# One scale for three tokens, a bound from sums, and a block's operand made within one block

## The chip, the cores and the metric

The kernel runs on one core of a Trainium2 chip. TensorE (PE) multiplies matrices into PSUM, VectorE (DVE), ScalarE (ACT) and GpSimd (POOL) do the element work, and SyncE (SP) issues most DMAs. Each engine takes its instructions in program order; between engines, semaphores order them. Measured is the device time of one execution in microseconds (us). The kernel before takes 1029.41 us, the median of three runs (1028.08 to 1030.17).

## The reference

Three stages on 4 batches of 4224 tokens with 192 channels.

```python
out = np.einsum('hk,bskhg->bshg', softmax(weight), windows(x))   # a causal 7-tap filter per head
u = x + (xT @ U @ V)T                                            # token mixing of rank 32
x = u + np.maximum(u @ w_ch1, 0.0) @ w_ch2                       # 192 -> 768 -> 192, first layer pair
u = x + np.real(np.fft.fft(np.fft.fft(x, axis=1), axis=2))
un = (u - mean(u)) / np.sqrt(var(u) + 1e-06)                     # per token
out = u + np.maximum(un @ w_ch1, 0.0) @ w_ch2                    # second layer pair
```

## The kernel before

**Blocks.** Both layer pairs work on blocks of 384 tokens: 128 partitions with three tokens each (`TB` = 3). There are 11 blocks in a batch and 88 in all, (s, b, j): s = 0 for the first layer pair and s = 1 for the second, b the batch. The order is (0,0), (0,1), (0,2), (1,0), (0,3), (1,1), (1,2), (1,3), 11 blocks each, so that blocks 0 to 32 and 44 to 54 have s = 0. Block i is the i-th of them.

**One block's life.** `pre1` (s = 0) or `pre2` (s = 1) makes the operand of the first layer. For s = 0: `add` puts the token mixing on `u` (matmuls `h`, then DVE, L525 or L534), `sizes` sums |u| of each token on ACT (L543), `scales` makes of the sums a scale per token on DVE (`cmax`, `rc`, L547 and L550), `high` scales `u` to `un` (ACT, L555) and rounds it to 16 bits in `sp` (L578), `low` takes the rest `un - sp` on POOL (L561), and a DMA transpose on SP (L585) turns `sp` into `ch`, channels on partitions. There is one buffer for `sp` and two for `ch`. For s = 1 `stats`, `root` and `normal` make mean and root of each token (L596 to L619), then come `high` (L625, L578) and `low` (L631; on DVE for 10 blocks). `layer1` multiplies `ch` with the first weights, six PSUM banks `l`, each evicted by ACT (`hh`, L650) and DVE (`hl`, L651). `layer2` multiplies `hh` and `hl` with the second weights, one token column r at a time (L697, L699, L701), and DVE adds the result to `u` (L704). After the third column of an s = 0 block DVE takes the largest |u| (L712) for the FFT's scale, and SP stores `u` to `x2d`, twice for j < 6; for s = 1 it stores the output.

**The order.** The program is written out by the loop at the end of `build`. In block i's turn r runs from 0 to 2: two of `layer1(i)`'s six units, then one unit of `layer2(i-1)`, then `fill`, which plays a share of the background units: the filter's matmuls and their evictions (`cv`, L398 and L404), the second weights' decoding on DVE (`dec`, L172 to L179), and the FFT (`fold`, `split33`, `s33`, `sd`, `s128`, `adds`), which gathers rows of `x2d` by DMAs that POOL issues (`xm`, L756). The preparation of block i+2 is laid among these: for s = 0 `add` in turn i at r = 0 and 1, `sizes` at r = 1 and 2, `scales` at r = 2, `high` and `low` in turn i+1 at r = 0 (in `PAIRED` stretches, where six `layer1` units stand together at r = 0, at the end of turn i). For s = 1: `stats` at r = 0, `root` and `normal` at r = 1, `high` and `low` at r = 2. `START` orders the first 29 steps by hand.

Of the kernel before, what the change touches and what calls it, by code (L numbers as in the profile page):

```python
# [20 lines left out]
P = 128  # L21
# [21 lines left out]

PAIRED = [(5, 11), (22, 34), (76, 88)]
# [53 lines left out]
def build(tc, io):  # L98
# [30 lines left out]
    with tc.manual_schedule():  # L129
# [319 lines left out]
        vsc = cst.tile([P, 2], F32, name="vsc")  # L449
        vst = cst.tile([96, 12, TB * P], F16, name="vst")  # L450
# [57 lines left out]
        def pre1(b, j):  # L508
            k = blk_t[0, b, j]
            u = k["u"]  # L510
            plain = b not in gst

            def add(r0, n):
                if plain:

                    if r0 == 0:
                        o = []
                        for r in range(TB):
                            t = TB * j + r
# [25 lines left out]
            def scales():  # L545
                c = k["cs"]
                nc.vector.tensor_scalar(out=c, in0=c, scalar1=1e-30, scalar2=1.0 / 8000.0,  # L547
                                        op0=ALU.max, op1=ALU.mult)
                rc = k["rc"] = wrk.tile([P, TB], F32, name="rc")
# [38 lines left out]
        def pre2(b, j):  # L588
# [3 lines left out]
            def stats():  # L592
                st = wrk.tile([P, TB, 6], F32, name="st")
                mv = wrk.tile([P, TB, 2], F32, name="mv", bufs=3)
                for r in range(TB):
                    nc.vector.bn_stats(out=st[:, r], in_=u[:, r])  # L596
                for r in range(TB):
                    nc.vector.bn_aggr(out=mv[:, r], in_=st[:, r])
                v = wrk.tile([P, TB], F32, name="va", bufs=1)
                nc.vector.tensor_scalar(out=v, in0=mv[:, :, 1], scalar1=1e-6, scalar2=None,  # L600
                                        op0=ALU.add)
                k["mv"], k["va"] = mv, v

            def root():
                s = k["s"] = wrk.tile([P, TB], F32, name="sd", bufs=1)
                nc.scalar.activation(s, k["va"], AF.Sqrt)

            def normal():
                mv, v, s = k["mv"], k["va"], k["s"]
                r = wrk.tile([P, TB], F32, name="rs", bufs=1)  # L610
                nc.vector.reciprocal(r, s)
                nc.vector.tensor_tensor(out=s, in0=r, in1=r, op=ALU.mult)
                nc.vector.scalar_tensor_tensor(out=s, in0=s, scalar=-16.0, in1=v,
# [21 lines left out]
            return [(None, stats), (root, normal), (high, low), (None, None)]  # L635
# [46 lines left out]
        def layer2(s, b, j):  # L682
# [6 lines left out]
            def unit(r):  # L689
# [16 lines left out]
                if final:  # L706
                    nc.sync.dma_start(io["out"][b][:, j * TB + r], u[:, r])
# [17 lines left out]
        def fft_units(b):  # L725
# [11 lines left out]
            def scale2():  # L737
# [3 lines left out]
                                        scalar2=2.0 ** -13, op0=ALU.max, op1=ALU.mult)  # L741
                nc.vector.reciprocal(m[:, 13:14], m[:, 12:13])
                nc.vector.tensor_scalar(out=m[:, 14:15], in0=m[:, 12:13], scalar1=2.0 ** 11,
# [63 lines left out]
            def s33(c, e):  # L807
# [17 lines left out]
                for a, n, o in ((1 + 3 * g0, 3 * nn, 0), (0, ng - nn, 102 * nn)):  # L825
                    if n:
# [3 lines left out]
                        nc.scalar.activation(hi, v, AF.Identity, scale=2.0 ** -11)  # L830
                        nc.vector.scalar_tensor_tensor(out=lo, in0=v, scalar=2.0 ** -11, in1=hi,
# [110 lines left out]
        def ahead(i):  # L942
            if i >= nblk:
                return [(None, None)] * 4
# [75 lines left out]
        def play(t):  # L1020
            for q in START[t].split() if t < len(START) else ():
                if q in jobs:
                    jobs[q]()
                else:
                    if q[0] in "ab" and q[0] not in queues:
                        queues[q[0]] = [f for e in ahead("ab".index(q[0])) for f in e]
# [30 lines left out]
        last, pre = None, [(None, None)] * 4  # L1057
        for i in range(nblk + 1):
            l1 = layer1(*blocks[i]) if i < nblk else [lambda: None] * NM
            old, pre = pre, ahead(i + 2)  # L1060

            soon = any(n < nblk and in_pairs(*blocks[n]) for n in (i + 1, i + 2))
            for r in range(TB):
                now = ([old[TB]] if r == 0 else []) + [pre[r]]
                l1[2 * r]()
                l1[2 * r + 1]()
                run(f for f, _ in now)
# [5 lines left out]
                run(f for _, f in now)  # L1073
                fill(TB * i + r)
            if soon:
                run(pre[TB])
                pre = pre[:TB] + [(None, None)]
# [60 lines left out]
```

## Time and profile before

| | |
|---|---|
| median of 3 runs | 1029.41 us (1028.08 to 1030.17) |
| the profiled execution: span from first to last instruction | 1017.3 us (its time beyond the span is not in the profile; the median is 12.1 us above the span) |
| PE busy | 979.1 us, 96% |
| DVE, ACT, POOL busy | 748.4 us (74%), 604.4 us (59%), 380.9 us (37%) |
| DMA engines | 45.6% of the span for the queue of SP and ACT, mean 137 GB/s in all |

PE's busy time counts from a matmul's start to its modelled end, so matmuls overlap: in a full stretch a matmul with 192 columns starts every 0.08 us and one with 384 every 0.16 us. What PE lost shows as idle time, in square brackets behind the instruction that ended it, with the work that released it, and as stretches with a lower granted clock.

### The profile page before, as it was taken

To read this page: it belongs to the slowest core of one execution; us is meant where nothing else is said; L and a number is where in the kernel's file an instruction comes from. 1 tells how busy PE (TensorE), PEld (TensorE's weight loads), DVE (VectorE), ACT (ScalarE), POOL (GpSimd) and SP (SyncE) were. 2 spreads that over 40 slices of the span, in tenths; PEclk is the share of its full clock that TensorE was granted. 3 is DMA by queue.
4 is the path that set the end of the run, shared out by engine and by line. 5 is a ranking of instruction groups with operands and counts; after the bars stand their busy time and mean duration, and the time that the engine had idled before them with its cause. 6 is when DMAs were issued, how large, how long until landed. Compare 5 with 4: busy or idle time off the path is not lost.

```text
span 1017.3 us, 25682 instructions
## 1 busy us (share of the span) xinstructions
PE 979.1 (96%) x9929; PEld 764.8 (75%) x9929; DVE 748.4 (74%) x2094; ACT 604.4 (59%) x1512; POOL 380.9 (37%) x397
## 2 busy tenths in 40 slices
PE   8789898999899999999999999998999999999998
PEld 5466676777677777877778887776888877877776
DVE  7766577689876656687776777897789787766663
ACT  2556554765676666656576666655656665555552
POOL 0111111253552344265534445564157651562110
PEclk9999999999999999999999999999999999999999
DMA  7596857685536666443425455433344332542332
GB/s 288 155 230 183 252 148 189 178 213 158 151 99 154 203 201 179 114 138 101 102 73 146 134 155 139 108 87 82 87 131 110 107 87 65 137 110 68 82 72 63
DMA packets 190804, 139.28 MB, mean 137 GB/s; under 512 B 128186, under 2 KB 164257, under 8 KB 189913
## 3 DMA queue, kind: packets, MB, share of 16 engines
q1 hardware_dynamic: 183095, 124.59, 45.6%
q0 software_dynamic: 7104, 12.70, 4.8%
q8 instruction: 77, 1.26, 0.5%
q14 instruction: 46, 0.38, 0.1%
q10 hardware_dynamic: 482, 0.35, 0.1%
HBM read 61.69 MB, written 46.11 MB: 106 GB/s over the span
## 4 chain that ended last, share of the span: by engine, by line
PE 62%; DVE 12%; DMA 11%; POOL 5%; issue 5%; ACT 4%; SPq 0%; DVEq 0%; ACTq 0%; POOLq 0%
PE l L665 24%; PE l L697 9%; PE l L701 8%; PE l L699 8%; PE l L655 5%; DMA ch<-sp 4%; DVE hl L651 3%; DMA xm<-x2d,mrow 2%; POOL xm L756 2%; PE cv L398 2%; PE sd L863 2%; PE s L879 2%; DMA x1d<-xw 1%; DVE x L790 1%; POOL xp L804 1%
## 5 line engine op out<-in xcount | busy, mean ns | idle before, releaser
L665 PE MATMUL l<-ch,w1h 128*128 128x384 f16 x1584 | 407.2, 327 | 15.4 <-DMA ch<-sp 10.1
L697 PE MATMUL l<-w2h,hh 128*128 128x192 f16 x1584 | 391.9, 247 | 5.8 <-DVE hl L651 4.5
L699 PE MATMUL l<-w2l,hh 128*128 128x192 f16 x1584 | 391.4, 247 | 1.2 <-DVE w2l L264 1.2
L701 PE MATMUL l<-w2h,hl 128*128 128x192 f16 x1584 | 391.4, 247 | 0.5 <-DVE hl L651 0.4
L651 DVE SCALAR_TENSOR_TENSOR hl<-l,hh 128x384 f16<-128x384 f32 x528 | 267.6, 549 | 127.2 <-ACT hh L650 126.1
L650 ACT ACTIVATE hh<-l 128x384 f16<-128x384 f32 x528 | 235.3, 494 | 155.7 <-PE l L655 155.3
L665 PEld LDWEIGHTS <-w1h 128*128 128x128 f16 x1584 | 155.1, 98 | 106.8 <-DMA ch<-sp 12.3
L697 PEld LDWEIGHTS <-hh 128*128 128x128 f16 x1584 | 155.6, 98 | 23.1 <-issue 12.3
L665 PE MATMUL l<-ch,w1l 128*128 128x384 f16 x528 | 172.7, 327 | 0.0
L699 PEld LDWEIGHTS <-hh 128*128 128x128 f16 x1584 | 155.7, 98 | 17.1 <-issue 6.5
L701 PEld LDWEIGHTS <-hl 128*128 128x128 f16 x1584 | 155.7, 98 | 3.1 <-DVE hl L651 1.4
L561 POOL TENSOR_TENSOR sp<-un,sp 128x576 f16<-128x576 f32 x44 | 57.3, 1302 | 250.4 <-ACT sp L578 228.3
L655 PE MATMUL l<-ch,w1l 128*128 128x384 f16 (+1 forms) x528 | 133.9, 327 | 0.0
L756 POOL DMA_INDIRECT xm<-x2d,mrow x84 | 84.9, 1011 | 21.3 <-issue 17.8
L631 POOL TENSOR_TENSOR sp<-un,sp 128x576 f16<-128x576 f32 x34 | 44.9, 1320 | 120.2 <-ACT sp L578 118.9
L625 ACT ACTIVATE un<-u,mr,rs 128x192 f32<-128x192 f32 x132 | 62.4, 537 | 25.3 <-DVE mr L619 24.7
L555 ACT ACTIVATE un<-u,rc 128x192 f32<-128x192 f32 x132 | 50.2, 445 | 43.0 <-DVE rc L550 43.0
L704 DVE SCALAR_TENSOR_TENSOR u<-l,cmax,u 128x192 f32<-128x192 f32 x132 | 54.5, 413 | 25.5 <-PE l L701 20.9
L665 PEld LDWEIGHTS <-w1l 128*128 128x128 f16 x528 | 51.8, 98 | 28.0 <-issue 4.0
L543 ACT ACTIVATE junk<-u 128x192 f16<-128x192 f32 x132 | 47.7, 361 | 40.6 <-DVE u L534 24.2
L849 POOL DMA_INDIRECT u<-x2d,mrow x64 | 62.4, 975 | 15.3 <-issue 11.7
L704 DVE SCALAR_TENSOR_TENSOR u<-l,ws,u 128x192 f32<-128x192 f32 x132 | 53.9, 410 | 18.2 <-PE l L701 18.0
(136 smaller groups left out, 1189.5 us busy)
## 6 DMA issues: line engine op xcount, KB each, us to landing
x2d<-u SPq DMA_DIRECT2D x68, 288.0 KB
u<-x1d SPq DMA_DIRECT2D x44, 288.0 KB
out_d<-u SPq DMA_DIRECT2D x43, 288.0 KB
x1d<-xw SPq DMA_DIRECT2D x36, 210.0 KB
u<-x2d SPq DMA_DIRECT2D x32, 192.0 KB
x<-x2d SPq DMA_DIRECT2D x60, 99.0 KB
xw<-x_d SPq DMA_DIRECT2D x4, 1344.0 KB
xw<-x_d SPq DMA_DIRECT2D x8, 672.0 KB
```

The costliest lines, as they stand in the source:

```text
L561: low_engine(0, b, j).tensor_tensor(out=sp[:, :, D:2 * D], in0=k["un"], in1=sp[:, :, :D], op=ALU.subtract)
L625: nc.scalar.activation(un[:, t], u[:, t], AF.Identity, scale=k["r"][:, t:t + 1], bias=k["m"][:, t:t + 1])
L650: nc.scalar.activation(hh[:, m], acc[m], AF.Relu)
L651: nc.vector.scalar_tensor_tensor(out=hl[:, m], in0=acc[m], scalar=0.0, in1=hh[:, m], op0=ALU.max, op1=ALU.subtract)
L655: nc.tensor.matmul(acc[m].rearrange("p (r n) -> p r n", r=TB), lhsT=w["l1"][rows, n, m * P:(m + 1) * P], rhs=kd[x][rows], start=False, sto ...
L665: nc.tensor.matmul(o, lhsT=w[v][:, e, ms], rhs=kd[x], start=(n == 0), stop=False)
L697: nc.tensor.matmul(o, lhsT=hh[:, m, rs], rhs=w["h2"][:, m], start=(m == 0), stop=False)
L699: nc.tensor.matmul(o, lhsT=hh[:, m, rs], rhs=w["l2"][:, m], start=False, stop=False)
L701: nc.tensor.matmul(o, lhsT=hl[:, m, rs], rhs=w["h2"][:, m], start=False, stop=(m == NM - 1))
L704: nc.vector.scalar_tensor_tensor(out=u[:, r], in0=o, scalar=sc, in1=u[:, r], op0=ALU.mult, op1=ALU.add)
L756: nc.gpsimd.indirect_dma_start(out=xs[c][1][:, g], out_offset=None, in_=x2d[b][:], in_offset=bass.IndirectOffsetOnAxis(ap=mrow[:99, k:k + ...
L849: nc.gpsimd.indirect_dma_start(out=u2[:, s0 + 2 * e], out_offset=None, in_=src[:], in_offset=bass.IndirectOffsetOnAxis(ap=mrow[:, k2 + e - ...
```

## The change

The turn of a block now has twelve slots: slot 4r comes after the first `layer1` unit of r, 4r + 1 after the second, 4r + 2 after `layer2`'s unit, 4r + 3 after `fill`. `SLOTS` says in which slot each piece of the preparation of block i+2 stands, and no number in it reaches 12.

- s = 0: one scale for a partition's three tokens. `sizes`, `scales` and `high` become one instruction each over 576 elements, where `sizes` and `high` had three. `add` stands in slot 5, `sizes` and `scales` in 7, `high` in 9 and `low` in 10.
- s = 1: `stats` in slot 0, `root` and `normal` in 4, `high` and `low` in 9. The constant 1e-6 goes into the root as a bias, and one small DVE instruction (L600) goes.
- `layer2`: the first two columns share a PSUM bank and are added by one DVE instruction of 384 elements after the second; the third as before. The last block's output leaves in two stores, not three.
- The FFT's bound is a sum of |u| by ACT instead of a largest |u| by DVE; two powers of two change with it.

```diff
+SLOTS = [(5, 5, 7, 7, 9, 10), (0, 4, 4, 9, 9)]
...
-            def sizes(r0, n):
-
-                if r0 == 0:
-                    k["cs"] = wrk.tile([P, TB], F32, name="cmax", bufs=5)
-                junk = wrk.tile([P, D], F16, name="junk", bufs=1)
-                for r in range(r0, r0 + n):
-                    nc.scalar.activation(junk, u[:, r], AF.Abs, accum_out=k["cs"][:, r:r + 1])
+            def sizes():
+                k["cs"] = wrk.tile([P, 1], F32, name="cmax", bufs=5)
+                junk = wrk.tile([P, TB * D], F16, name="junk", bufs=1)
+                nc.scalar.activation(junk, u.rearrange("p r d -> p (r d)"), AF.Abs,
+                                     accum_out=k["cs"])
...
-                for r in range(TB):
-                    nc.scalar.activation(un[:, r], u[:, r], AF.Identity,
-                                         scale=k["rc"][:, r:r + 1])
+                nc.scalar.activation(un.rearrange("p r d -> p (r d)"),
+                                     u.rearrange("p r d -> p (r d)"), AF.Identity,
+                                     scale=k["rc"])
...
-            return [(None, lambda: add(0, 2)), (lambda: sizes(0, 2), lambda: add(2, 1)),
-                    (lambda: sizes(2, 1), scales), (high, low)]
+            return list(zip(SLOTS[0], (lambda: add(0, 2), lambda: add(2, 1), sizes, scales, high, low)))
...
-            return [(None, stats), (root, normal), (high, low), (None, None)]
+            return list(zip(SLOTS[1], (stats, root, normal, high, low)))
...
-                ps = psm("l2")
-                o = ps[:, :D]
+                if r != 1:
+                    k["l2"] = psm("l2")
+                o = k["l2"][:, D:2 * D] if r == 1 else k["l2"][:, :D]
...
-                sc = k["cs"][:, r:r + 1] if s == 0 else w["ws"]
-                nc.vector.scalar_tensor_tensor(out=u[:, r], in0=o, scalar=sc, in1=u[:, r],
-                                               op0=ALU.mult, op1=ALU.add)
+                sc = k["cs"] if s == 0 else w["ws"]
+                if r:
+                    a = 2 * (r - 1)
+                    v = u[:, a:r + 1].rearrange("p r d -> p (r d)")
+                    nc.vector.scalar_tensor_tensor(out=v, in0=k["l2"][:, :(r + 1 - a) * D],
+                                                   scalar=sc, in1=v, op0=ALU.mult, op1=ALU.add)
...
-                        nc.vector.tensor_reduce(out=xmax[b][:, j:j + 1],
-                                                in_=u.rearrange("p r d -> p (r d)"), axis=AX.X,
-                                                op=ALU.max, apply_absolute_value=True)
+                        junk = wrk.tile([P, TB * D], F16, name="junk", bufs=1)
+                        nc.scalar.activation(junk, u.rearrange("p r d -> p (r d)"), AF.Abs,
+                                             accum_out=xmax[b][:, j:j + 1])
...
             for r in range(TB):
-                now = ([old[TB]] if r == 0 else []) + [pre[r]]
                 l1[2 * r]()
+                at(4 * r)
                 l1[2 * r + 1]()
-                run(f for f, _ in now)
+                at(4 * r + 1)
                 play(TB * i + r + 1)
...
-                run(f for _, f in now)
+                at(4 * r + 2)
                 fill(TB * i + r)
+                at(4 * r + 3)
```

Three places in the order of the instructions. On POOL before, from the gathers around block 17's preparation on; `un_3687` is block 18's, `xm` the FFT's gathered rows.

```order
L804 TENSOR_TENSOR xp_3523<-xm_2988,xp_3523 99x768
L756 DMA xm_3399<-x2d0_70,mrow_78 99x192 x2
L795 TENSOR_TENSOR xm_3399<-x33_3398 99x4x95
L756 DMA xm_3661<-x2d0_70,mrow_78 99x192 x2
L561 TENSOR_TENSOR sp_84<-un_3687,sp_84 128x3x192
L804 TENSOR_TENSOR xp_3768<-xm_3399,xp_3768 99x768
```

The same place on POOL now; block 18's is `un_3503`.

```order
L806 TENSOR_TENSOR xp_3415<-xm_2897,xp_3415 99x768
L758 DMA xm_3296<-x2d0_70,mrow_78 99x192 x2
L562 TENSOR_TENSOR sp_86<-un_3503,sp_86 128x3x192
L797 TENSOR_TENSOR xm_3296<-x33_3295 99x4x95
L758 DMA xm_3560<-x2d0_70,mrow_78 99x192 x2
L806 TENSOR_TENSOR xp_3653<-xm_3296,xp_3653 99x768
```

The subtraction of block 18 has moved in front of the FFT's `fold` (L795, now L797) and two gathers.

On DVE before, in turn 5, where the second weights' first piece has just been decoded (its last instruction is L223); `rc_1577` is block 7's scale.

```order
L223 TENSOR_REDUCE mx1_1482<-u2_1474 128x1
L122 TENSOR_REDUCE vsc_82<-am_1548 128x1
L464 TENSOR_SCALAR vsc_82<-vsc_82 128x1
L466 RECIPROCAL vsc_82<-vsc_82 128x1
L704 SCALAR_TENSOR_TENSOR u_673<-l2_1553,cmax_902,u_673 128x192
L712 TENSOR_REDUCE xmax_821<-u_673 128x1
L547 TENSOR_SCALAR cmax_1484<-cmax_1484 128x3
L550 RECIPROCAL rc_1577<-cmax_1484 128x3
L651 SCALAR_TENSOR_TENSOR hl_1592<-l1_1593,hh_1591 128x384
```

The same place on DVE now; block 7's scale is `rc_1493`.

```order
L224 TENSOR_REDUCE mx1_1435<-u2_1427 128x1
L548 TENSOR_SCALAR cmax_1489<-cmax_1489 128x1
L551 RECIPROCAL rc_1493<-cmax_1489 128x1
L123 TENSOR_REDUCE vsc_82<-am_1514 128x1
L467 TENSOR_SCALAR vsc_82<-vsc_82 128x1
L469 RECIPROCAL vsc_82<-vsc_82 128x1
L706 SCALAR_TENSOR_TENSOR u_668<-l2_1519,cmax_907,u_668 128x192
L649 SCALAR_TENSOR_TENSOR hl_1549<-l1_1550,hh_1548 128x384
```

The scale stands directly behind the decoded piece, five instructions sooner, and the reduction L712 is no longer on DVE; the decoding is ahead of it as before.

On SP before, at the end of turn 12; `ch_2910` is block 14's operand, `u_1985` block 11.

```order
L716 DMA x2d1_71<-u_1985 128x576 x2
L504 DMA u_2863<-x1d1_67 128x576
L585 DMA_TRANSPOSE ch_2910<-sp_84 128x9x128
L368 DMA x1d2_68<-xw_2119 56x4x192 x2
L773 DMA x33_2987<-x2d0_70 33x4x192 x3
```

The same place on SP now.

```order
L718 DMA x2d1_71<-u_1930 128x576 x2
L585 DMA_TRANSPOSE ch_2778<-sp_86 128x9x128
L507 DMA u_2786<-x1d1_67 128x576
L369 DMA x1d2_68<-xw_2058 56x4x192 x2
L775 DMA x33_2718<-x2d0_70 33x4x192 x3
```

The transpose has moved in front of the load of a later block and stands right behind the two stores.

## Rows read from the trace of the kernel before

**Rows 1.** The page: busy time, share of the span and instructions of three engines.

```profile
PE 979.1 (96%) x9929; PEld 764.8 (75%) x9929; DVE 748.4 (74%) x2094; ACT 604.4 (59%) x1512; POOL 380.9 (37%) x397
```

**Rows 2.** What PE waited for: total us, times, longest us.

```profile
PE l L665 <- DMA ch<-sp: 10.1, 10, 2.8
```

**Rows 3.** PE's timeline: start, us, instruction, in brackets the idle time and its end.

```profile
42.20 0.32 PE L665 MATMUL l<-ch,w1h 128*128 128x384 f16 x1 [2.67 <-DMA ch<-sp]
...
65.78 0.34 PE L665 MATMUL l<-ch,w1h 128*128 128x384 f16 x1 [1.30 <-DVE xmax L712]
...
77.16 0.34 PE L665 MATMUL l<-ch,w1h 128*128 128x384 f16 x1 [0.34 <-DMA ch<-sp]
...
124.86 0.32 PE L697 MATMUL l<-w2h,hh 128*128 128x192 f16 x1 [3.37 <-DVE hl L651]
...
165.34 0.24 PE L697 MATMUL l<-w2h,hh 128*128 128x192 f16 x1 [1.16 <-DVE hl L651]
...
169.74 0.34 PE L665 MATMUL l<-ch,w1h 128*128 128x384 f16 x1 [1.18 <-DMA ch<-sp]
...
193.02 0.44 PE L398 MATMUL cv<-xw,tap 64*64 64x168 f32 x4 [1.03 <-DMA xw<-x_d]
...
267.08 0.50 PE L665 MATMUL l<-ch,w1h 128*128 128x384 f16 x1 [2.83 <-DMA ch<-sp]
...
991.04 0.34 PE L665 MATMUL l<-ch,w1h 128*128 128x384 f16 x1 [0.45 <-DVE u L704]
```

**Rows 4.** Three stretches: us, busy us of PE, PEld, DVE, ACT, POOL, clock, DMA share.

```profile
123.20:130.00 6.80, 5.14 (x42) 3.88 (x42) 4.95 (x10) 4.58 (x11) 1.53 (x2) 0.50 0.69 179
130.00:266.60 136.60, 129.09 (x1393) 100.16 (x1391) 106.71 (x284) 84.39 (x231) 41.91 (x38) 1.00 0.64 172
266.60:270.00 3.40, 2.92 (x10) 1.41 (x11) 2.22 (x9) 0.49 (x1) 1.71 (x2) 0.50 0.93 301
```

**Rows 5.** ACT's timeline at 257 us, block 18's rounding.

```profile
257.07 0.68 ACT L578 ACTIVATE sp<-un 128x576 f16<-128x576 f32 x1
```

**Rows 6.** POOL's timeline from 251 to 264 us.

```profile
251.25 1.00 POOL L756 DMA_INDIRECT xm<-x2d,mrow  x1 [0.30 <-issue]
258.68 1.23 POOL L795 TENSOR_TENSOR xm<-x 99x380 f32<-99x380 f32 x1 [6.43 <-DVE xm L791]
...
262.44 1.30 POOL L561 TENSOR_TENSOR sp<-un,sp 128x576 f16<-128x576 f32 x1
```

**Rows 7.** DVE's timeline in turn 5.

```profile
117.57 0.26 DVE L172 TENSOR_SCALAR dec<-u 128x192 int32<-128x192 int32 x1 [3.41 <-DMA u<-wa_d]
...
119.31 0.35 DVE L223 TENSOR_REDUCE mx<-u 128x1 f32<-128x192 f32 x1
...
121.46 0.17 DVE L550 RECIPROCAL rc<-cmax 128x3 f32<-128x3 f32 x1
```

**Rows 8.** ACT's timeline in turn 5.

```profile
121.72 1.15 ACT L555 ACTIVATE un<-u,rc 128x192 f32<-128x192 f32 x3 [6.64 <-DVE rc L550]
...
123.74 0.47 ACT L650 ACTIVATE hh<-l 128x384 f16<-128x384 f32 x1
```

**Rows 9.** Groups by line and shape: count, busy us, mean ns, idle before us.

```profile
L704 DVE SCALAR_TENSOR_TENSOR u<-l,cmax,u 128x192 f32<-128x192 f32 x132 | 54.5, 413 | 25.5 <-PE l L701 20.9 <-PE gp L414 0.5
L712 DVE TENSOR_REDUCE xmax<-u 128x1 f32<-128x576 f32 x44 | 33.1, 753 | 1.5
L534 DVE SCALAR_TENSOR_TENSOR u<-h,gm,u 128x384 f32<-128x384 f32 x33 | 20.1, 608 | 0.4 <-PE s L879 0.2
...
L578 ACT ACTIVATE sp<-un 128x576 f16<-128x576 f32 x88 | 60.1, 683 | 3.1 <-DMA ch<-sp 0.4
L543 ACT ACTIVATION_READ_ACCUMULATOR junk<-u 128x1 f32 x132 | 25.2, 191 | 0.0
```

**Rows 10.** SP's timeline at 57 us, a transpose's issue.

```profile
57.62 5.38 SPq L585 DMA_TRANSPOSE ch<-sp  x1
```

**Rows 11.** The page's DMA issues: count and KB each.

```profile
x2d<-u SPq DMA_DIRECT2D x68, 288.0 KB
```

More of the change, by code (lines that the diff above doesn't have):

```diff
@@ L449, in build @@
         vsc = cst.tile([P, 2], F32, name="vsc")
+        eps = cst.tile([P, 1], F32, name="eps")
+        nc.gpsimd.memset(eps, 1e-6)
         vst = cst.tile([96, 12, TB * P], F16, name="vst")
@@ L548, in scales @@
                                         op0=ALU.max, op1=ALU.mult)
-                rc = k["rc"] = wrk.tile([P, TB], F32, name="rc")
+                rc = k["rc"] = wrk.tile([P, 1], F32, name="rc")
                 nc.vector.reciprocal(rc, c)
@@ L598, in stats @@
                     nc.vector.bn_aggr(out=mv[:, r], in_=st[:, r])
[L599 to L602, printed above, removed]
+                k["mv"] = mv
             def root():
                 s = k["s"] = wrk.tile([P, TB], F32, name="sd", bufs=1)
-                nc.scalar.activation(s, k["va"], AF.Sqrt)
+                nc.scalar.activation(s, k["mv"][:, :, 1], AF.Sqrt, bias=eps)
             def normal():
-                mv, v, s = k["mv"], k["va"], k["s"]
+                mv, s = k["mv"], k["s"]
                 r = wrk.tile([P, TB], F32, name="rs", bufs=1)
                 nc.vector.reciprocal(r, s)
-                nc.vector.tensor_tensor(out=s, in0=r, in1=r, op=ALU.mult)
-                nc.vector.scalar_tensor_tensor(out=s, in0=s, scalar=-16.0, in1=v,
+                nc.vector.scalar_tensor_tensor(out=s, in0=mv[:, :, 1], scalar=1e-6, in1=r,
+                                               op0=ALU.add, op1=ALU.mult)
+                nc.vector.scalar_tensor_tensor(out=s, in0=s, scalar=-16.0, in1=r,
                                                op0=ALU.mult, op1=ALU.mult)
@@ L702, in unit @@
                                      stop=(m == NM - 1))
-                sc = k["cs"][:, r:r + 1] if s == 0 else w["ws"]
-                nc.vector.scalar_tensor_tensor(out=u[:, r], in0=o, scalar=sc, in1=u[:, r],
-                                               op0=ALU.mult, op1=ALU.add)
-                if final:
-                    nc.sync.dma_start(io["out"][b][:, j * TB + r], u[:, r])
+                sc = k["cs"] if s == 0 else w["ws"]
[4 more added lines that the diff above has]
+                                                   scalar=sc, in1=v, op0=ALU.mult, op1=ALU.add)
+                    if final:
+                        nc.sync.dma_start(io["out"][b][:, j * TB + a:j * TB + r + 1], u[:, a:r + 1])
                 if r == TB - 1:
@@ L740, in scale2 @@
                 nc.vector.tensor_scalar(out=m[:, 12:13], in0=m[:, 12:13], scalar1=1e-30,
-                                        scalar2=2.0 ** -13, op0=ALU.max, op1=ALU.mult)
+                                        scalar2=2.0 ** -14, op0=ALU.max, op1=ALU.mult)
                 nc.vector.reciprocal(m[:, 13:14], m[:, 12:13])
-                nc.vector.tensor_scalar(out=m[:, 14:15], in0=m[:, 12:13], scalar1=2.0 ** 11,
+                nc.vector.tensor_scalar(out=m[:, 14:15], in0=m[:, 12:13], scalar1=2.0 ** 5,
                                         scalar2=None, op0=ALU.mult)
@@ L829, in s33 @@
                                   [:, :, a:a + n] for l in range(2)]
-                        nc.scalar.activation(hi, v, AF.Identity, scale=2.0 ** -11)
-                        nc.vector.scalar_tensor_tensor(out=lo, in0=v, scalar=2.0 ** -11, in1=hi,
+                        nc.scalar.activation(hi, v, AF.Identity, scale=2.0 ** -5)
+                        nc.vector.scalar_tensor_tensor(out=lo, in0=v, scalar=2.0 ** -5, in1=hi,
                                                        op0=ALU.mult, op1=ALU.subtract)
@@ L943, in ahead @@
             if i >= nblk:
-                return [(None, None)] * 4
+                return []
             s, b, j = blocks[i]
@@ L1025, in play @@
                     if q[0] in "ab" and q[0] not in queues:
-                        queues[q[0]] = [f for e in ahead("ab".index(q[0])) for f in e]
+                        queues[q[0]] = [f for _, f in ahead("ab".index(q[0]))]
                     for _ in range(int(q[1:] or 1)):
@@ L1055, in fill, with at @@
                     done[n] = upto
-        last, pre = None, [(None, None)] * 4
+        last, pre = None, []
         for i in range(nblk + 1):
             l1 = layer1(*blocks[i]) if i < nblk else [lambda: None] * NM
-            old, pre = pre, ahead(i + 2)
+            pre = [(n - 12, f) for n, f in pre if n >= 12] + ahead(i + 2)
+            def at(n):
+                run(f for m, f in pre if m == n)
             soon = any(n < nblk and in_pairs(*blocks[n]) for n in (i + 1, i + 2))
             for r in range(TB):
-                now = ([old[TB]] if r == 0 else []) + [pre[r]]
                 l1[2 * r]()
+                at(4 * r)
                 l1[2 * r + 1]()
-                run(f for f, _ in now)
+                at(4 * r + 1)
                 play(TB * i + r + 1)
@@ L1072, in build @@
                     last[r]()
-                run(f for _, f in now)
+                at(4 * r + 2)
                 fill(TB * i + r)
+                at(4 * r + 3)
             if soon:
-                run(pre[TB])
-                pre = pre[:TB] + [(None, None)]
+                run(f for n, f in pre if n >= 12)
+                pre = []
             ahead_load(i + 4)
```

2 rows, old and new, of the table START are left out of this document.

## The prediction

> **What bounds the kernel now.** I read the busy shares first. PE is busy in 96% of the span, DVE in 74%, ACT in 59% [rows 1]. So the change, which takes no matmul away, can only win what PE loses by waiting, 1017.3 - 979.1 = 38.2 us, and what it loses to a lower clock. Second, PE's waits by releaser: 10.1 us in ten waits are for the transposed operand `ch` [rows 2], the largest single releaser. Third, where these waits lie: PE's timeline has six over 1 us that the change may touch, 1.30 us at 65.78, 3.37 at 124.86, 1.16 at 165.34, 1.18 at 169.74, 1.03 at 193.02 and 2.83 at 267.08; behind them come seven under 0.6 us before a block's first matmul, from 0.34 at 77.16 to 0.45 at 991.04, 2.7 us together [rows 3]. Fourth, the granted clock. It is 1.00 nearly everywhere (130.0 to 266.6 is such a stretch), but 0.50, 1.2 GHz for 2.4, from 123.2 to 130.0 and from 266.6 to 270.0, each right at a long idle of PE [rows 3, 4]. Work in these stretches runs at half speed, so they cost half their length, 3.4 and 1.7 us.
>
> **The operand sooner (s = 0).** Take 267.08. ACT had rounded block 18 by 257.07 + 0.68 = 257.75 us [rows 5], but POOL's subtraction began at 262.44: POOL stood in order in front of the FFT's fold, which waited 6.43 us for DVE until 258.68, and two gathers [rows 6]. From the subtraction's end at 263.74 to PE's matmul at 267.08 went 3.3 us. In the changed order the subtraction stands in front of that fold, right behind the gathers that were done at 252.25 [rows 6], and its own inputs are made in the turn before. So it ends some 8 us sooner, the operand lands long before PE asks for it, and the 2.83 us go. What is late next is the eviction of block 17, which DVE makes no later than before. With the idle goes its reason for the low clock, 1.7 us. The waits at 65.78 and 169.74 are the same kind, an operand made just in time: 1.30 + 1.18. PE's wait at 65.78 carries DVE's L712 as releaser; that instruction leaves DVE, and the transpose moves in front of a load on SP, so either cause is gone. Of the seven small waits four lie in s = 0, where the operand comes some half a turn sooner, and three in s = 1, where only `normal` moves; I take 2.2 of their 2.7 us. The xw load that ends the wait at 193.02 was queued on SP behind a transpose that now comes sooner; how far the load's own buffer allows it no row shows, so 0 to 1.03, and I take 0.5. Sum of this part: 2.83 + 1.7 + 1.30 + 1.18 + 2.2 + 0.5 = 9.7 us; bounds 4 (large waits half closed, no clock) and 10.7.
>
> **Less on DVE, in front of the evictions.** In an s = 0 block three additions of 413 ns and a reduction of 753 ns become additions of 608 (the 384-element row of L534) and 413 ns [rows 9]: 1.99 us become 1.02. In an s = 1 block the additions save 0.22. That is 44 x 0.97 + 44 x 0.22 = 52 us of DVE's 748. Off the path it is worth nothing; PE hides it. It counts where DVE sets PE's wait, at 124.86. There DVE waits 3.41 us for the second weights' DMA until 117.57, decodes until 119.66, and reaches block 7's scale at 121.46 [rows 7]; ACT starts `high` at 121.72 and the evictions of block 6 only at 123.74 [rows 8], and PE needs a bank that they free. The scale now stands right behind the decoded piece: 119.66 plus two short instructions, about 120.0. `high` is one instruction instead of three in 1.15 us [rows 8]; the same 576 elements take 683 ns in L578 [rows 9], a per-partition scale may add some, say 0.7. With 0.95 us of rounding ACT is free at 121.7. But in front of the evictions it now has the sum for the bound, 683 + 191 ns [rows 9], and so reaches them at 122.5, 1.2 us sooner. The decoding and its DMA are not moved. Of the 3.37 us 1.2 go (bounds 0.3, if the sum waits for the last column, and 2.1, if it is hidden). The clock's 3.4 us then hang on an idle of 2.2 us: all or nothing, and the nearest rows lie on both sides, 2.83 us with the drop and 2.67 at 42.20 without [rows 3]; I take half, 1.7. At 165.34 the same order, with no DMA, should close all of 1.16. Sum 4.1 us; bounds 1.5 and 6.7.
>
> **What it adds.** The sum for the bound makes ACT wait in every s = 0 block for DVE's last addition; behind it stand the filter's evictions and the next block's first `hh`. PE has by then two further `layer1` units (ten matmuls of 0.16 us) and a `layer2` unit of an older block (18 of 0.08) in its queue, 3 us of work, and that covers 0.87 us. Uncovered it would be 44 x 0.87 = 38 us; with a margin of 2 us per block I take 0. On DVE `scales` now waits for ACT's `sizes` in slot 7; what is queued behind it is the eviction of unit 4, whose `hh` ACT makes after `sizes` anyway: 0. The shared bank is held from column 0 to column 1, but a block takes one bank fewer, and where six units stand together column 0 was evicted only after six `hl` before too: 0. The tail: the last store stands behind a store of two columns rather than one, 0.2 us.
>
> The Trainium skill ("ScalarE: Activation LUTs", Rules for kernel authors) says that a maximum belongs on VectorE, which is faster per element, and so speaks against this move. The rows agree on the price of one, 874 ns for 753, but not on the place: DVE is the fuller engine. If ACT bounded, the rule would make the move cost 44 x 0.12 = 5.3 us and the sum 1022.8.
>
> **The sum.** 9.7 + 4.1 - 0.2 = 13.6 us. PE will reach the waits that the change does not touch (gathers, filter loads) that much sooner, and some will grow; I give back 1.6 and take 12. The profiled span is 1017.3 and would be 1005.3; the median stands 12.1 us above the span, and I carry that over: 1029.4 - 12.0 = 1017.4 us.
>
> **Rivals.** *Half is lost again:* the closed idle comes back as longer waits for gathers, weights and filter loads, whose times DMA sets. For it: DVE's wait in turn 5 is for a DMA [rows 7], and the xw wait is one [rows 3]. Against: the loads are issued in program order behind work that moves with PE. 6 us stay: 1023.4.
>
> *More closes:* both low clocks go, and the relieved DVE shortens the FFT's and the start's waits too. 10.7 + 6.7 and some 3 us more: 20 us, 1009.
>
> *Slower: the transposes queue behind the stores.* In s = 0 the transpose now stands on SP right behind the stores to `x2d`, 2 x 288 KB [rows 11] in the 24 blocks with j < 6. At the 172 GB/s of a usual stretch [rows 4] these 576 KB take 3.3 us. `sp` has one buffer, so a loop runs through every block: stores 3.3, transpose 3.3, rounding 0.68, subtraction 1.30, together 8.6 us against 1017.3 / 88 = 11.6 us for a block. It decides from 3 us more on. For it: one transpose behind other traffic took 5.38 us for its issue alone [rows 10]; 4 us of that, 12.6 for 11.6, would hold ACT's rounding and with it the next evictions 1 us in each of 24 blocks: 24 - 12 = 12 us slower, 1041. Against: that one stood behind the weights' and the filter's first transfers, in the fullest stretch. The Trainium skill ("DMA: Bandwidth & Descriptors", Queues, rings and completion order) has each DMA engine consume descriptors in ring order; by that the 3.3 us are paid in every such block, and whether more is, no row shows.
>
> *It does nothing:* the waits are set by something that the rows name wrongly, as at 65.78, and new ones replace them: 1029.
>
> **Chances.** The forecast's case (7 to 17 us faster) 0.57, half lost 0.18, more closes 0.06, nothing 0.06, slower 0.13. A measurement of this kernel can tell 0.2%, 2.1 us, from no change. Faster by more: 0.57 + 0.18 + 0.06 = 0.81; within: 0.06; slower: 0.13. The likeliest case alone spans 1012 to 1023. The range goes from 1008 (more closes) to 1030, where nothing is still inside and slower is left out.
>
> **What would show it.** Right: in the changed profile no wait over 0.5 us for `ch` after 60 us; POOL's subtraction of block 18 before the fold; PE's clock 1.00 around the former 267 us; the wait behind the first decoded piece near 2 us; DVE's busy time near 696 us and ACT's no higher. Wrong: ACT idle before the sum for the bound with PE idle right behind it; a transpose's issue of several us in most s = 0 blocks, with ACT's L578 waiting for `ch`; or PE's idle as large as before under other releasers.

## The result, and the profile after

The changed kernel takes 1002.77 us, the median of four runs (1000.67 to 1004.68), and the kernel before, beside it, 1029.79 (1028.08 to 1031.99). The ratio is 0.9735, with a 95% interval of 0.9715 to 0.9755: 27 us faster, where 12 were forecast. The direction was right; the time lies below the range.

The page of the changed kernel, busy time by engine, which answers to [rows 1]:

```profile
span 999.7 us, 25272 instructions
PE 972.6 (97%) x9929; PEld 761.5 (76%) x9929; DVE 684.3 (68%) x1918; ACT 593.8 (59%) x1336; POOL 380.9 (38%) x398
```

PE is idle or waiting for 27.1 us of the span, not 38.2, and its busy time fell by 6.5 us with not a matmul fewer; 13.6 us less at 1.2 GHz (the stretches below) would save 6.8. DVE lost 64 us, ACT 11. The profiled execution took 1001.54 us, 1.84 more than its span.

What PE waited for (total us, times, longest), the first of them the line of [rows 2]; the second has no counterpart before, and the third stands in the turn that had 1.16 us at 165.34:

```profile
PE l L663 <- DMA ch<-sp: 2.7, 2, 2.2
...
PE l L698 <- issue: 2.3, 3, 1.1
...
PE h L533 <- DVE hl L649: 1.8, 1, 1.8
```

The 10.1 us in ten waits for `ch` are 2.7 in two, and 2.2 of these stand at 41.52 us, in front of the program's first block. PE's timeline, in the places of [rows 3] and at the largest waits that are left:

```profile
48.92 0.32 PE L663 MATMUL l<-ch,w1h 128*128 128x384 f16 x1 [2.54 <-DVE hl L649]
...
57.55 0.24 PE L698 MATMUL l<-w2l,hh 128*128 128x192 f16 x1 [0.16 <-DVE w2l L265]
...
116.96 0.24 PE L696 MATMUL l<-w2h,hh 128*128 128x192 f16 x1 [0.51 <-DVE hl L649]
...
155.72 0.24 PE L533 MATMUL h<-gst,vst 96*128 96x192 f16 x1 [1.76 <-DVE hl L649]
...
209.87 0.24 PE L698 MATMUL l<-w2l,hh 128*128 128x192 f16 x1 [0.58 <-issue]
...
431.10 0.25 PE L698 MATMUL l<-w2l,hh 128*128 128x192 f16 x1 [1.05 <-issue]
...
675.95 0.43 PE L825 MATMUL s<-vt,xp 99*97 99x102 f16 x5 [1.43 <-POOL xp L806]
```

The waits of 3.37 and 2.83 us are 0.51 and nothing. The 1.16 us at 165.34 have become 1.76, a wait for a PSUM bank that DVE has to empty. New are pieces that no releaser ends ("issue", 5.5 us in all after 38 us), in the middle of runs of matmuls.

The stretches of [rows 4]; columns as there:

```profile
49.86:53.28 3.41, 3.41 (x14) 1.62 (x13) 2.51 (x9) 2.13 (x5) 0.00 (x0) 0.50 0.90 232
53.28:998.70 945.42, 928.83 (x9484) 734.01 (x9482) 644.65 (x1814) 573.85 (x1290) 376.57 (x388) 1.00 0.50 135
```

One stretch at half clock is left, behind the idle at 48.92, and none until the tail. In the profile before there were four, of 17 us together (at 58, 123, 267 and 693 us).

POOL's timeline, for [rows 6]. The subtraction of block 18 now comes before the fold (line 797) and not behind it:

```profile
244.94 1.38 POOL L562 TENSOR_TENSOR sp<-un,sp 128x576 f16<-128x576 f32 x1 [3.46 <-ACT sp L578]
248.57 1.24 POOL L797 TENSOR_TENSOR xm<-x 99x380 f32<-99x380 f32 x1 [2.25 <-DVE xm L793]
```

Turn 5 on DVE and ACT, for [rows 7, 8]:

```profile
110.56 0.26 DVE L173 TENSOR_SCALAR dec<-u 128x192 int32<-128x192 int32 x1 [1.23 <-DMA u<-wa_d]
...
112.75 0.16 DVE L551 RECIPROCAL rc<-cmax 128x1 f32<-128x1 f32 x1
```

```profile
113.01 0.78 ACT L555 ACTIVATE un<-u,rc 128x576 f32<-128x576 f32 x1 [4.31 <-DVE rc L551]
...
115.16 0.68 ACT L715 ACTIVATE junk<-u 128x576 f16<-128x576 f32 x1
...
115.83 2.39 ACT L648 ACTIVATE hh<-l 128x384 f16<-128x384 f32 x6
```

The scale stands right behind the decoded piece, as forecast, and from the load's landing to ACT's first eviction are 5.27 us for 6.17 (0.9 less; 1.2 were forecast). But the load itself lands 0.5 us before block 6's first matmul (111.10) and no longer 1.4 us behind it. On SP, whose rows of the kernel before stand first here, the order is the same before and now: the stores, block 6's transpose, a load of tokens, the weights' load. But before, SP stood at the transpose from 104.40 to 108.04 us; now it is issued with no wait behind the stores:

```profile
103.59 0.81 SPq L716 DMA_DIRECT2D x2d<-u  x2
108.04 1.52 SPq L585 DMA_TRANSPOSE ch<-sp  x1
112.14 0.32 SPq L504 DMA_DIRECT2D u<-x1d  x1
112.51 0.43 SPq L201 DMA_DIRECT2D u<-wa_d  x1
```

```profile
98.55 0.81 SPq L718 DMA_DIRECT2D x2d<-u  x2
99.53 2.16 SPq L585 DMA_TRANSPOSE ch<-sp  x1
104.59 0.32 SPq L507 DMA_DIRECT2D u<-x1d  x1
105.36 0.34 SPq L202 DMA_DIRECT2D u<-wa_d  x1
```

The weights' load was issued 3.6 us before block 6's first matmul, and now 5.7. What SP stood for is POOL's subtraction of block 6, which ended 3.6 us behind the stores' issue (108.01 for 104.40) and now ends 0.3 us before that issue does (99.01 for 99.36); POOL before, then now:

```profile
106.73 1.28 POOL L561 TENSOR_TENSOR sp<-un,sp 128x576 f16<-128x576 f32 x1 [7.31 <-ACT sp L578]
```

```profile
97.73 1.28 POOL L562 TENSOR_TENSOR sp<-un,sp 128x576 f16<-128x576 f32 x1 [5.26 <-ACT sp L578]
```

Block 9's turn, the place of the 1.16 us at 165.34, on ACT before and now:

```profile
164.23 2.38 ACT L650 ACTIVATE hh<-l 128x384 f16<-128x384 f32 x6
```

```profile
153.31 0.68 ACT L715 ACTIVATE junk<-u 128x576 f16<-128x576 f32 x1 [1.52 <-DVE u L706]
...
153.99 2.37 ACT L648 ACTIVATE hh<-l 128x384 f16<-128x384 f32 x6
```

ACT reaches the evictions 6.5 us after PE's first matmul of block 9 (157.77, now 147.54), no sooner than before: it now stands 1.52 us for DVE's last addition, which the sum for the bound reads.

### The profile page after: what moved, and what is told of

Same layout as the page of the kernel before. It is cut to its first block, busy times and chain, and to the rows that moved or that the text cites. A ratio compares the mean times of both kernels' runs of the same rounds, so it can differ in the third digit from the quotient of the medians.

```text
span 999.7 us, 25272 instructions
## 1 busy us (share of the span) xinstructions
PE 972.6 (97%) x9929; PEld 761.5 (76%) x9929; DVE 684.3 (68%) x1918; ACT 593.8 (59%) x1336; POOL 380.9 (38%) x398
## 4 chain that ended last, share of the span: by engine, by line
PE 73%; DVE 8%; DMA 7%; issue 5%; POOL 3%; ACT 3%; SPq 0%; DVEq 0%; POOLq 0%; ACTq 0%
PE l L663 27%; PE l L696 11%; PE l L700 10%; PE l L698 10%; PE l L653 6%; PE cv L399 2%; DMA xm<-x2d,mrow 2%; DMA x1d<-xw 2%; PE sd L865 2%; DVE hl L649 2%; PE s L881 2%; POOL xm L758 2%; PE s L825 1%; DVE x L792 1%; DMA ch<-sp 1%
## 5 line engine op out<-in xcount | busy, mean ns | idle before, releaser
L649 DVE SCALAR_TENSOR_TENSOR hl<-l,hh 128x384 f16<-128x384 f32 x528 | 270.4, 548 | 155.7 <-ACT hh L648 143.0
L758 POOL DMA_INDIRECT xm<-x2d,mrow x84 | 84.6, 1007 | 21.3 <-issue 18.1
L653 PEld LDWEIGHTS <-w1l 128*128 128x128 f16 (+1 forms) x528 | 40.4, 97 | 34.2 <-issue 9.9
L578 ACT ACTIVATE sp<-un 128x576 f16<-128x576 f32 x88 | 60.1, 683 | 3.1 <-DMA ch<-sp 0.4
L543 ACT ACTIVATE junk<-u 128x576 f16<-128x576 f32 x44 | 30.0, 681 | 44.2 <-issue 20.0
L706 DVE SCALAR_TENSOR_TENSOR u<-l,ws,u 128x384 f32<-128x384 f32 x88 | 44.2, 510 | 13.8 <-PE l L700 7.8
```

The lines of the kernel that those rows point to most:

```text
L578: nc.scalar.activation(sp[:, :, :D], k["un"], AF.Identity)
L649: nc.vector.scalar_tensor_tensor(out=hl[:, m], in0=acc[m], scalar=0.0, in1=hh[:, m], op0=ALU.max, op1=ALU.subtract)
L653: nc.tensor.matmul(acc[m].rearrange("p (r n) -> p r n", r=TB), lhsT=w["l1"][rows, n, m * P:(m + 1) * P], rhs=kd[x][rows], start=False, sto ...
L758: nc.gpsimd.indirect_dma_start(out=xs[c][1][:, g], out_offset=None, in_=x2d[b][:], in_offset=bass.IndirectOffsetOnAxis(ap=mrow[:99, k:k + ...
```

## The experiments

Fifteen runs were made, in four groups, each group on one chip. "Before" and "changed" below are the two kernels; a ratio is to the runs of before in the same group.

**The base: before, once more.** No edit.

> The kernel before, unchanged. The profiled execution had a span of 1017.3 us, the timed runs a median of 1029.8, and the profile of the changed kernel has 1.84 us around its span (1001.54 for 999.7). Theory one: the 12 us are the fixed time around the span of the kernel before; then each run here has about 12 us around its span and spans near 1017. Theory two: about 1.8 us lie around every span, and the timed runs of before have spans of 1026 to 1030; then a new profile should show PE's idle or its low-clock stretches longer by some 10 us in all than the first profile (38.2 us idle, clock 0.50 in four stretches of 3.4 to 6.8 us), and the waits of before are not the same from run to run.

1029.94 us beside 1030.68, ratio 0.9986 (0.9969 to 1.0004); span 1027.8 for 1029.62. Theory two: about 1.8 us lie around each span, and the span of the profile that the prediction used was 10.5 us shorter than this one. Up to 430 us the two agree within 3.5 us; then this one loses 12. PE's timeline:

```profile
442.72 0.24 PE L701 MATMUL l<-w2h,hl 128*128 128x192 f16 x1 [0.92 <-issue]
...
812.66 0.32 PE L665 MATMUL l<-ch,w1h 128*128 128x384 f16 x1 [0.83 <-DVE z L831]
...
817.18 0.67 PE L823 MATMUL s<-vt,xp 99*97 99x102 f16 x10 [1.16 <-POOL xp L804]
...
828.78 0.67 PE L823 MATMUL s<-vt,xp 99*97 99x102 f16 x10 [0.95 <-POOL xp L804]
...
878.40 0.20 PE L863 MATMUL sd<-vt,z 95*128 95x97 f16 x1 [1.13 <-issue]
```

> The kernel before, one more profile. The second profile lost 10.5 us to the first, nearly all after 430 us: pieces of PE idle without a releaser near 443, 540, 773 and 878 us (5.0 us), a chain of late gathers at 812 to 840 us (3.4 us) and a low clock near 696 us. Theory usual: these stand in most executions of before, so this span is 1025 to 1032 and they are there again. Theory accident: they come and go, and this span lies between 1017 and 1028 with other waits.

> The changed kernel, unchanged, on the chip of this call. If the first profile (span 999.7 us) is a usual execution, as its four times of 1000.7 to 1004.7 say, the time is 1000 to 1005 us, the waits at 117, 144, 156, 279 and 676 us stand again within 0.5 us, and the idle pieces without a releaser (5.5 us in all) may move. If the changed kernel too has executions 10 us apart, the span or the idle after 440 us differs by several us from the first profile's.

In this group, on another chip, before took 1016.86 us (its third profile has a span of 1015.0) and the changed kernel 992.94, ratio 0.9756 (0.9737 to 0.9776). The times expected did not come: not 1000 to 1005 us for the changed kernel, and not a span of before of 1025 to 1032 or 1017 to 1028. Each theory named a cause within a chip; but both kernels differ from group to group, so it is the chip, or something else that lasts as long as a group. Idle without a releaser after 38 us is 0.0 in both profiles here, and 5.0 us in the second of before and 5.5 in the first of the changed kernel. The groups with the references `after_third` and `after_fourth` had 1028.56 and 1001.77, and 1015.84 and 994.27.

> The changed kernel, unchanged, as the reference of this call. Two chips have been seen: one gives 1030.7 us for the kernel before and 1002.8 for the changed one, with 5 to 7.5 us of PE idle that no releaser ends; the other 1016.9 and 992.9, with none. Theory chip: this call's chip is one of these two kinds, and PE's idle without a releaser is again near 5 us or near 0, with the time of the kernel before on the same side.

> The changed kernel, unchanged, as the reference of this call: 1000 to 1005 us on a chip of the slower kind, 991 to 996 on one of the faster.

In `after_third` that idle is 4.3 us, in `after_fourth` 0.0: two chips of each kind, as expected. By this sign and its span (1017.3, none of that idle) the first profile of before is of the faster kind, while its timed runs are of the slower.

**Operations and order apart.** The changed kernel's operations in the old order, twice:

```
-SLOTS = [(5, 5, 7, 7, 9, 10), (0, 4, 4, 9, 9)]
+SLOTS = [(2, 6, 9, 10, 13, 14), (2, 5, 6, 9, 10)]
```

> The changed kernel's operations (one scale for three tokens, sums for the bound on ACT, constant in the root, two columns evicted together) at the places where the kernel before had them: the operand is prepared over two blocks as before. My prediction's terms give these operations part of 4.1 us: about 1026. Theory order (the operand a step sooner makes the gain): 1022 to 1030, PE's waits near 125, 170 and 267 us remain above 1 us. Theory less work (DVE's shorter queue makes the gain): 1005 to 1012, and those waits are gone.

> The new operations at the places of the kernel before once more, beside the changed kernel on one chip. Theory both are needed: 15 to 22 us above the changed kernel, with waits for ch of 1 to 3 us at about 65, 77, 225, 262, 286, 489 and 639 us. Theory chip (the operations alone gain more where PE has no idle of its own): within 10 us of it.

1022.94 us, ratio 0.9932 (0.9906 to 0.9958), and on another chip 1019.82, 0.9919 (0.9893 to 0.9944): 8 us gained of 27. The waits for `ch` stay. PE's timeline in the first of the two (in the second the middle wait, 2.23 us at 261.83, carries `ch` as its releaser):

```profile
64.51 0.34 PE L663 MATMUL l<-ch,w1h 128*128 128x384 f16 x1 [2.83 <-DMA ch<-sp]
...
261.95 0.34 PE L663 MATMUL l<-ch,w1h 128*128 128x384 f16 x1 [2.18 <-DVE gm L345]
...
285.63 0.50 PE L663 MATMUL l<-ch,w1h 128*128 128x384 f16 x1 [2.42 <-DMA ch<-sp]
```

And the old operations in the new order (three scales, three evictions, the maximum on DVE, the addition before the root); `SLOTS`, the second layer's list and the loop are those of the changed kernel:

```
...
-            return [(None, lambda: add(0, 2)), (lambda: sizes(0, 2), lambda: add(2, 1)),
-                    (lambda: sizes(2, 1), scales), (high, low)]
+            return list(zip(SLOTS[0], (lambda: add(0, 2), lambda: add(2, 1), lambda: sizes(0, TB), scales, high, low)))
...
```

> The operations of the kernel before, in the changed order (prepared and transposed within one block). My prediction's terms: 9.7 us and the part of 4.1 that the scale's place makes, about 1018. Theory order: 1003 to 1012, no wait for ch over 0.5 us after 60 us. Theory less work: 1020 to 1029. If both are needed (a just-in-time chain that either relieves), this and the run with the operations alone each show more than half of the 27 us.

1018.32 us, ratio 0.9872 (0.9847 to 0.9897): 12 us. No wait for `ch` over 0.5 us after 60 us, as forecast; but PE now waits for DVE:

```profile
158.60 0.24 PE L531 MATMUL h<-gst,vst 96*128 96x192 f16 x1 [2.76 <-DVE hl L651]
...
188.07 0.44 PE L399 MATMUL cv<-xw,tap 64*64 64x168 f32 x4 [1.94 <-DVE xmax L712]
...
258.41 0.32 PE L697 MATMUL l<-w2h,hh 128*128 128x192 f16 x1 [2.56 <-DVE z L831]
```

8 and 12 us apart make 20; together they are 27. That either edit alone shows more than half, the last case of the expectation, did not come: they do more together than apart. The starts of the blocks say where the rest is made. Up to block 20 (some 280 us), against the second profile of before, the operations gain 2.9 us, the order 0.7, both together 13.2. From there to the end they gain 6.9, 10.9 and 15.0. So early on each is worth little without the other: order alone trades waits for `ch` for waits for DVE, and operations alone relieve a DVE that PE is mostly not waiting for. The 1018 us expected of the order alone came by luck: the prediction's terms for it lie mostly before 290 us, and there it gained 0.7.

**How much is DVE's relief?** The second layer's additions one column at a time again and the maximum on DVE again (its powers of two with it), both undone, then each by itself:

```
...
-                sc = k["cs"] if s == 0 else w["ws"]
-                if r:
...
+                nc.vector.scalar_tensor_tensor(out=u[:, r], in0=o, scalar=sc, in1=u[:, r],
+                                               op0=ALU.mult, op1=ALU.add)
...
```

```
-                        nc.scalar.activation(junk, u.rearrange("p r d -> p (r d)"), AF.Abs,
-                                             accum_out=xmax[b][:, j:j + 1])
+                        nc.vector.tensor_reduce(out=xmax[b][:, j:j + 1],
+                                                in_=u.rearrange("p r d -> p (r d)"), axis=AX.X,
+                                                op=ALU.max, apply_absolute_value=True)
...
```

> The changed kernel with the last two columns evicted one by one on DVE again and the bound a maximum on DVE again; the order, the single scale and the constant in the root stay. DVE's busy time goes from 684 to about 736 us. Theory order: 1002 to 1006. Theory less work: 1010 to 1020, and the wait near 117 us is again over 2 us with a low clock behind it. My prediction's terms: up to 4.1 us, 1007.

> The changed kernel with the last two columns evicted by two additions (two of 0.41 us for one of 0.61, 88 times, 19 us of DVE's busy time); the bound's sum stays on ACT. The bound's maximum alone cost 4.5 us on the faster chip and the two together 9.1 on the slower. If the costs add, 3 to 6 us above the changed kernel; if only the maximum counts, within 2 us of it.

> The changed kernel with only the bound's sum back on DVE as a maximum (44 x 0.75 us). Both edits that relieve DVE in the eviction path, undone together, cost 9 us. Theory maximum (the reduction, last in DVE's row before the filter's work, holds it): 1008 to 1012. Theory evictions (two columns in one addition): 1002 to 1005. My prediction's terms, a saving off the path: within 2 us of the changed kernel.

Both undone: 1011.87 us, ratio 0.9823 (0.9793 to 0.9853), 9 us above the changed kernel's first result, by the times and by the ratios. The order alone took 1018.32 on the same chip, so what this run keeps of the operations, one scale and the constant in the root, is worth 6.5 us in the new order. Evictions alone: 1006.98 beside 1001.77, 5.2 us. The maximum alone: 997.39 beside 992.94, 4.5 us with a wide spread (995.67 to 1003.01), near the 5 to 9 of its first theory and not within the 2 of the prediction's terms. The costs add. With the evictions undone PE waits where the order alone made it wait, for DVE's `z`, an eviction of the FFT, in front of the second layer:

```profile
251.44 0.24 PE L695 MATMUL l<-w2h,hh 128*128 128x192 f16 x1 [1.38 <-DVE z L829]
...
274.26 0.24 PE L695 MATMUL l<-w2h,hh 128*128 128x192 f16 x1 [1.33 <-DVE z L829]
```

With the maximum undone, the wait for a bank that is 1.76 us in the changed kernel is longer, and 3.4 us at half clock follow; PE's timeline and that stretch:

```profile
156.50 0.32 PE L533 MATMUL h<-gst,vst 96*128 96x192 f16 x1 [2.57 <-DVE hl L649]
```

```profile
156.08:159.49 3.41, 2.99 (x20) 2.75 (x19) 3.41 (x9) 0.00 (x0) 0.00 (x0) 0.50 1.05 281
```

In the two other kernels this wait is 2.76 us (both undone) and 1.98 (evictions), with 3.4 us at half clock behind it too; none of the changed kernel's four profiles, with 1.76 to 1.78 us, has one there. The wait near 117 us, which the expectation of `dve_off` named, did not come back. The Trainium skill's rule that a maximum belongs on VectorE ("ScalarE: Activation LUTs", Rules for kernel authors) does not hold here as a choice of place: putting it back there costs 4.5 us, since DVE's row, for which PE waits there, and not the price of one, decides.

**The second layer's order.** Its five pieces at their old slots, `(2, 5, 6, 9, 10)`.

> The changed kernel with the first layer's blocks in the changed order and the second layer's at their places before (slots 2, 5, 6, 9, 10 for stats, root, normal, high, low). My prediction puts nearly all of the order's gain in the first layer: within 2 us of the changed kernel, 1002 to 1005. Rival: the second layer's order holds a share, then 1006 to 1015, and the waits after 450 us (for ch at 489, 639 us as before) come back.

995.94 us beside 992.94: 3.0 us, between the 2 expected and the rival's 3 to 12. Of the rival's signs a wait for `ch` is back, 0.87 us at 471 us, in front of block 38.

**Sooner still.** All pieces one slot sooner, `[(4, 4, 6, 6, 8, 9), (0, 3, 3, 8, 8)]`:

> The changed kernel with the preparation one slot sooner still: first layer (4, 4, 6, 6, 8, 9), second (0, 3, 3, 8, 8). Only one wait for ch over 0.5 us is left after 60 us (2.2 us at 74 us, in one of two profiles). Theory order still pays: 1 to 3 us below the changed kernel, by that wait. Theory DVE's row decides now: the same within 2 us, or slower, as each piece stands in front of evictions that PE waits for (117, 156, 279 us).

1022.30 us beside 1001.77: 20.5 us lost, far more than either theory. Two kernels part the transpose from the rest: only the low part and its transpose sooner, `(5, 5, 7, 7, 9, 9)`, so that the transpose stands in front of the stores to `x2d`; and all sooner but the transpose, `(4, 4, 6, 6, 8, 10)`.

> The changed kernel with one number changed: the first layer's low part, with its transpose, in slot 9 instead of 10, so that the transpose stands on SP in front of the stores to x2d and not behind them. The operand is not later. Theory store (a transpose in front of the store holds SP until the rounding is there, the store leaves late, and the load that waits for it, and the weights' and the filter's loads behind that, land late): 12 to 20 us slower than the changed kernel, SP's waits of u<-x1d for x2d<-u near 80 us instead of 10 to 14, new waits for xw. Theory rows (the kernel with all pieces one slot sooner lost 20 us because its pieces stood in front of evictions on ACT and DVE): within 3 us of the changed kernel.

> All pieces one slot sooner, (4, 4, 6, 6, 8, .) and (0, 3, 3, 8, 8), but the first layer's low part and transpose back in slot 10, behind the stores. Theory store: within 4 us of the changed kernel. Theory rows: 15 to 20 us slower, like the kernel with all pieces sooner.

1009.47 us, 15.2 above 994.27, and 998.85, 4.6 above: theory store, with some 4.6 us for the other pieces. By the starts of the blocks 16.1 of the 16.9 us between the two profiles are lost before block 12 (some 200 us), where the weights' and the filter's loads stand behind the store. What SP's load of the next tokens waited for (total us, times, longest), in the changed kernel and with the transpose in front:

```profile
SPq L507 <- DMA x2d<-u: 16.6, 19, 2.6
```

```profile
SPq L507 <- DMA x2d<-u: 87.5, 39, 8.3
```

SP's timeline of the latter: the transpose waits for `sp`, the store behind it leaves only then, the load waits 8.3 us for that store, and the weights' load stands behind it, 1.8 us ahead of block 6's first matmul (119.30):

```profile
103.67 1.46 SPq L585 DMA_TRANSPOSE ch<-sp  x1
...
107.35 1.00 SPq L718 DMA_DIRECT2D x2d<-u  x2
...
116.73 0.32 SPq L507 DMA_DIRECT2D u<-x1d  x1
117.49 0.34 SPq L202 DMA_DIRECT2D u<-wa_d  x1
```

PE pays with waits for the filter's input and for the decoded piece:

```profile
115.31 0.68 PE L399 MATMUL cv<-xw,tap 64*64 64x120 f32 x7 [2.01 <-DMA xw<-x_d]
...
126.15 0.48 PE L663 MATMUL l<-ch,w1h 128*128 128x384 f16 x1 [4.09 <-DVE vsc L123]
```

No version tried beats the changed kernel.

## Why the prediction was wrong

The mechanism was right for the largest waits; the sum was half of what came. The fair measure is its own profile against one of the changed kernel on a chip of the same kind, `after_fourth`, with a span of 991.5 us: 25.8 us, by the starts of the blocks.

| stretch | forecast | measured |
|---|---|---|
| to block 6 (start, 65.78, 77.16) | 1.6 | 4.1 |
| block 6 (124.86 and its clock) | 2.9 | 5.2 |
| blocks 7 to 11 (165.34, 169.74, 193.02) | 2.8 | 1.9 |
| blocks 12 to 18 (267.08 and its clock) | 4.5 | 5.2 |
| from there to the end (other small waits, less 1.6 given back, less 0.2) | 0.1 | 9.4 |

With `before_third` and `after_again` in their places the five rows are 0.7, 2.8, 2.5, 5.0 and 10.3, 21.3 us in all: the last three are much the same, the first two differ from execution to execution (before, the wait in block 6 is 3.37 us in one profile and 2.2 and 2.3 in the others, with 3.4 us at half clock and not 6.8).

- **267.08: right**, the 2.83 us, the clock's 1.7, and the order as the cause: with the old order it stays 2.2 us, with the order alone it is gone. That it is POOL's order is read from the traces. The subtraction ends 7.3 us ahead of block 18's first matmul and not 3.3, some 4 us sooner where 8 were expected.
- **124.86: the step "The decoding and its DMA are not moved" failed.** Their places in the order are the same, but the transpose in front of the weights' load no longer waits 3.6 us for its operand, and the load lands 2.0 us sooner against block 6. That and the scale's 0.9 us make the 2.9 us by which the wait shrank. The idle left was 0.51 and not 2.2 us, and all 3.4 us of the clock went, not half.
- **165.34: the step "the same order, with no DMA, should close all of 1.16" failed**, and with it the 0 for the bound's sum: ACT waits there for DVE's last addition, and PE's 1.16 us became 1.76.
- **"Off the path it is worth nothing; PE hides it" failed.** DVE's relief was priced at two places of the old order. In the new order DVE is what is late next: with the order alone PE waits 2.56 us at 258.41, in block 17's turn, for DVE's `z`, where the prediction had looked at "the eviction of block 17, which DVE makes no later than before" alone. Undoing 49 of DVE's 64 us cost 9 us. Terms worked out one by one from the old trace missed what the edits give only together, some 7 us on the slower chips.
- **"I give back 1.6" had the wrong sign.** Between blocks 20 and 33 0.6 us were given back (a new wait of 1.03 us at 279); behind them 9.8 more closed. Of the waits of 1.1 to 1.2 us at 487.98 (`ch`, one of the ten of [rows 2], but in no term of the sum), 678.71 and 690.84 us (`xp`) one is left, of 0.4, and the low clock at 693 went, 1.7. These make 4.8 of the 9.8 us; how the rest divides was not followed. The rival "more closes" named relief of this kind at 1009 us and got 0.06; it was the right one, and still too small.
- **The clock** was given 3.4 us. Three of four stretches went, 13.6 us long: 6.8, as PE's busy time says (6.5). The one at 58 us moved to 50; in `after_fourth` none is left before the tail.
- **"I carry that over"** took the 12.1 us between median and span as fixed. They were 1.8 us and a chip of the other kind. This error cost little by itself: the slower chips gained 27 us in both groups, the faster 24 (1016.86 to 992.94) and 22 (1015.84 to 994.27), and 3 to 5 of the 15 us missed lie there.
- **Slower, transposes behind the stores:** it did not come; no transpose's issue takes over 3 us in the changed profile. One in `after_again` took 5.0 us at 65 us, and `ch` was 2.2 us late at 74. The stores' place does matter, the other way round: a transpose in front of them costs 15 us. The Trainium skill's ring order ("DMA: Bandwidth & Descriptors", Queues, rings and completion order) would have the 3.3 us paid in every such block; if they are, PE does not wait for them.
- **The signs:** POOL's order, the clock near 267, no `ch` wait over 0.5 us after 60 us, and ACT no higher held in the first profile. In `after_again` one `ch` wait of 2.2 us stood at 74 us. DVE was forecast at 696 and was 684, the wait behind the decoded piece near 2 us and was 0.51. One sign of being wrong came, in block 9's turn: ACT idle before the bound's sum with PE idle right behind it.

What stays open: how the 7 us that need both edits divide over single waits, what the one scale and the constant in the root are each worth, and why the first 80 us differ between executions of the changed kernel (waits of 2.5 us at 49 us in some, at 74 in one).

## What to carry to other kernels

When a change both moves an operand sooner and thins the row of the engine next in line, do not add terms from the old trace: ask of each closed wait what is late next, and whether the other edit closes that too. On an in-order queue ask what stands behind an instruction that has to wait; one slot was worth 15 us here, nearly all of it where loads stood behind a store. And compare a profile with timed runs only when both are of one chip.

## What the runs showed of the hardware

Chips differed by some 1.3%: the kernel before took 1030.7 and 1028.6 us on two, 1016.9 and 1015.8 on two others; each chip was met in one group of runs only. All seven profiles on the latter have 0.0 us of PE idle without a releaser after 38 us; the eight on the former have 4 to 7.5 us, near the same places of the program, with no wait on the instruction that comes late. In all eight, and in the first of the changed kernel, such pieces stand in the turns of blocks 33, 42, 64 and 73, though these begin 22 to 28 us apart from kernel to kernel: they go by the place in PE's program and not by the time. This idle makes some 5 of the 13 us; of the rest, late gathers were a part (3.4 us at 812 to 840 us in one profile). What holds PE there no view shows.
